# A retention layer feeding a feed-forward block: the halves of the last output slice loaded one place later, their casts moved behind two turned chunks, and products moved ahead of transposes

## The chip, the cores and the metric

The kernel runs on one core of one Trainium2 chip. The metric is device time in microseconds. Before the change the median of three runs is 191.54 us (191.42, 191.54 and 193.94 us). One further execution was profiled: it took 192.3 us, of which 190.5 us lie between its first and its last instruction (the span). All rows of a trace count from the start of that span.

## The reference

The first half is a recurrent attention over 768 steps, for 4 batches of 8 heads of width 64; the second is a feed-forward block over the 3072 resulting tokens.

```
state = gamma * state + outer(k[t], v[t])      # per batch and head, gamma = 1 - 2**(-5-h)
y[t]  = q[t] @ state / sqrt(64)
h     = y_tokens @ w_in                        # 3072 x 512 by 512 x 2048
g     = h * tanh(softplus(h))
out   = g @ w_out                              # 2048 x 512, float32 out
```

## The kernel before

The recurrence is done in chunks of 128 steps, numbered 0 to 23 over the four batches. For a chunk the kernel needs its q and k turned so that the head dimension lies on partitions ("qkt"), a product of both ("at", the scores), a mask ("am"), a product with v ("y"), and the state: an outer product of k and v ("u") added to the state of the chunk before ("suc") and decayed ("stc"). Chunks are gathered to blocks: the first block has four, and ten more have two each. For each block the feed-forward's two products follow, and in all blocks after the first both of them use a scheme of seven products instead of eight on quarter matrices, for which sums of operands are formed on VectorE ("xsum", "gsum", "wsum", "tmat").

The program is written in an order by hand: each engine executes its instructions in the order of the calls, and waits on semaphores where an operand or a buffer isn't ready. The place of the change is the end of the first block, the function `first_g2` (lines 1185 to 1307), which computes the first block's second product and, between its pieces, prepares chunks 4 to 7. `CPB` is 4, so `CPB` and `CPB + 1` are chunks 4 and 5, the two of the next block. What the names there mean:

- `mm(...)` in `first_g2` is four matmuls of 128 by 128 by 256 (line 1210). `pe[p]`, `px[p]`, `pz[p]`, `pb[p]` are accumulators in PSUM for the two token pairs p = 0 and 1; `sm(p, i)` are sums of activations, `t(i)` sums of weights, `a(p, i, s)` activations, `b(s, j)` output weights.
- `turn(g, True)` (line 449) transposes q and then k of chunk g by TensorE, four transposes each (lines 453 and 455), into a PSUM tile of the pool "at", and copies the tile out on ScalarE (line 458).
- `outer_fifth(CPB)` (line 599) is eight small matmuls for chunk 4's outer product (line 604) and an addition on VectorE (line 608); `decay_of_fifth` (line 610) is four small activations on ScalarE (line 614).
- `cast_wout(3, ...)` (line 209) casts a half of the last slice of output weights on ScalarE (line 214). The slice's halves are loaded by `load_last_wout` (line 194, 512 KB each) in `load_more`; the other loads there are q and v of chunks 5 to 7 (line 157, 256 KB each). All are issued by SyncE on one queue.
- k of a chunk is loaded by GpSimd's queue with a cast on the way (`bring_k`, lines 415 and 418); GpSimd also scales q (line 406) and v (line 423).
- `some_late(n)` takes the next n of a list of sums of output weights on VectorE (lines 722 to 725).
- `scores`, `mask` and `y_two` (lines 469, 565, 640 and 622) finish chunks 4 and 5; `end` (line 1275) multiplies with the last slice of output weights.

The PSUM pool "at" has two buffers, used in turn: both turned chunks, the outer product of chunk 4, the scores of 4 and of 5, y, each takes the next one, and waits until its last reader is done.

Of the kernel before, what the change touches and what calls it, by code (L numbers as in the profile page):

```python
# [16 lines left out]
def kernel(  # L17
# [176 lines left out]
    def load_last_wout(half):  # L194
        f = slice(half * (FPS // 2), (half + 1) * (FPS // 2))
        nc.sync.dma_start(
            wtmps["out", NSL - 1][:, f], wout_ap[:, NFB - FPS + f.start:NFB - FPS + f.stop])
# [11 lines left out]
    def cast_wout(s, f, on_act=False):  # L209
        if s not in wouts:  # L210
            wouts[s] = cpool.tile([P, FPS, d_model], FP16, name=f"wout{s}")
        dst, src = wouts[s][:, f], wtmps["out", s][:, f]
        if on_act:
            nc.scalar.copy(dst, src)
        else:
            nc.vector.tensor_copy(dst, src)
# [204 lines left out]
    def cast_v(g):  # L421
        if g < NCK:
            nc.gpsimd.tensor_tensor(  # L423
                room16(g)[2], loaded[g][2], vs.unsqueeze(2).broadcast_to((P, H, D)), op=ALU.mult)
# [24 lines left out]
    def turn(g, on_act=False):  # L449
        q16, k16 = cast[g][:2]  # L450
        t_ps = atps.tile([P, H, C], FP16, name="t_ps", tag="at")
        for i in range(HP):
            nc.tensor.transpose(t_ps[:, i], q16[:, 2 * i:2 * i + 2], ident)
        for i in range(HP):
            nc.tensor.transpose(t_ps[:, HP + i], k16[:, 2 * i:2 * i + 2], ident)
        qkt = qktp.tile([P, H, C], FP16, name="qkt", bufs=4)
        if on_act:
            nc.scalar.copy(qkt, t_ps)
        else:
            nc.vector.tensor_copy(qkt, t_ps)  # L460
        qkts[g] = (qkt[:, :HP], qkt[:, HP:])

    def scores(g):
        at = ats[g] = atps.tile([P, 2, HP, C], FP32, name="at", tag="at")
        qt, kt = qkts[g]
        for i in range(HP):
            for hh in range(2):
                o = 64 * hh
                nc.tensor.matmul(  # L469
                    at[:, hh, i], kt[o:o + 64, i], qt[o:o + 64, i],  # L470
                    start=True, stop=True)
# [127 lines left out]
    def outer_fifth(g):  # L599
        _, k16, v16, _ = cast[g]  # L600
        u_ps = u_tile()[:, 0, :, :D]
        for i in range(HP):
            for x in range(2):
                nc.tensor.matmul(
                    u_ps[64 * x:64 * x + 64, i], k16[:, 2 * i + x], v16[:, 2 * i + x],
                    start=i == 0, stop=True, skip_group_check=True)
        sus[g] = stp.tile([P, HP, D], FP32, name="suc", tag="suc")
        nc.vector.tensor_tensor(sus[g], u_ps, stcs[g - 1], op=ALU.add)

    def decay_of_fifth():  # L610
        stcs[CPB] = stp.tile([P, HP, D], FP16, name="stc", tag="stc")
        su = sus.pop(CPB)
        for i in range(HP):
            nc.scalar.activation(stcs[CPB][:, i], su[:, i], AF.Copy, scale=gcf[:, i:i + 1])
# [426 lines left out]
        load_one(CPB + 1, 0, nc.sync)  # L1041

    def load_more():
        load_last_wout(0)
        load_one(CPB + 1, 2, nc.sync)
        load_last_wout(1)
        nload[0] += 2
        room(CPB + 2)
        load_one(CPB + 2, 2, nc.sync)
        load_one(CPB + 2, 0, nc.sync)  # L1050
        nload[0] += 1
        load_to(CPB + 4)
# [132 lines left out]
    def first_g2():  # L1185
        hf = d_model // 2
        pairs = range(CPB // 2)
        t1 = [mmps.tile([P, 2, hf], FP32, name="o_ps", tag="mm") for _ in pairs]
        t0 = [mmps.tile([P, 2, hf], FP32, name="o_ps", tag="mm") for _ in pairs]
        osb = [[op.tile([P, 2, hf], FP32, name="osb", tag="osb") for _ in range(2)] for _ in pairs]  # L1190
        m5 = [op.tile([P, hf], FP32, name="snap", tag="snap", bufs=4) for _ in pairs]
        pb, pe = [t[:, 0] for t in t0], [t[:, 1] for t in t0]
        px, pz = [t[:, 0] for t in t1], [t[:, 1] for t in t1]
        sums = gsums[0].rearrange("p s (f a) t -> p s f (a t)", a=2)

        def a(p, i, s):
            return lambda f: gts[0, s * FPS + f][:, (2 * p + i) * P:(2 * p + i + 1) * P]

        def sm(p, i):
            return lambda f: sums[:, i - 1, f, p * P:(p + 1) * P]  # L1200

        def b(s, j):
            return lambda f: wouts[s][:, f, j * hf:(j + 1) * hf]

        def t(i):
            return lambda f: tmats[(i - 1) // 2][:, (i - 1) % 2, f]

        def mm(o_ps, x, w, first=False, last=False):
            for f in range(FPS):
                nc.tensor.matmul(  # L1210
                    o_ps, x(f), w(f), start=first and f == 0, stop=last and f == FPS - 1,
                    skip_group_check=True)

        for p in pairs:
            mm(px[p], a(p, 0, 0), b(0, 0), True)
            nc.scalar.copy(osb[p][0][:, 0], px[p])
        cast_wout(1, slice(3, 4), True)
        room_for_more()
        for p in pairs:
            mm(pe[p], sm(p, 1), t(1), True)  # L1220
            nc.scalar.copy(m5[p], pe[p])
        cast_wout(2, slice(0, 2))
        cast_wout(2, slice(2, 4), True)
        some_late(1)
        gate(tmats[0][:, 1, 0, :1])
        cast_q(CPB)
        cast_q(CPB + 1)
        cast_v(CPB)
        some_late(1)
        g_sum(4)  # L1230
        some_late(1)
        for p in pairs:
            mm(pz[p], a(p, 1, 1), b(1, 1))
        for p in pairs:
            mm(pb[p], a(p, 0, 1), b(1, 0))
        for p in pairs:
            mm(pb[p], a(p, 0, 2), b(2, 0))
        for p in pairs:
            mm(pe[p], a(p, 0, 1), b(1, 1))
        for p in pairs:  # L1240
            mm(px[p], sm(p, 2), t(2))
            nc.scalar.copy(osb[p][0][:, 1], px[p])
        turn(CPB, True)
        for p in pairs:
            mm(px[p], sm(p, 3), t(3))
            nc.vector.tensor_tensor(osb[p][1][:, 1], px[p], m5[p], op=ALU.add)
        bring_k(CPB + 2)
        cast_v(CPB + 1)
        cast_wout(3, slice(0, 2), True)
        for p in pairs:  # L1250
            mm(pe[p], sm(p, 4), b(2, 1))
            if p == 0:
                turn(CPB + 1, True)
        outer_fifth(CPB)
        some_late(1)
        decay_of_fifth()
        cast_wout(3, slice(2, 4), True)
        for p in pairs:
            mm(px[p], a(p, 1, 1), b(1, 0))
        scores(CPB)  # L1260
        scores(CPB + 1)
        mask(CPB)
        mask(CPB + 1)
        some_late(2)
        for p in pairs:
            mm(px[p], a(p, 1, 2), t(4))
        cast_v(CPB + 2)
        bring_k(CPB + 3)
        cast_q(CPB + 2)
        turn_by_dma(CPB + 2)  # L1270
        load_early_v(CPB + 4)

        def end(p, i, half):
            for f in range(2 * half, 2 * half + 2):
                nc.tensor.matmul(  # L1275
                    (t0, t1)[i][p], a(p, i, 3)(f), wouts[3][:, f], start=False,
                    stop=f == FPS - 1, skip_group_check=True)

        def ended(p, i):
            if i == 0:  # L1280
                nc.vector.tensor_tensor(osb[p][0], t0[p], osb[p][0], op=ALU.add)
            else:
                works = [
                    lambda: nc.vector.tensor_tensor(
                        osb[p][1][:, 1], pz[p], osb[p][1][:, 1], op=ALU.add),
                    lambda: nc.scalar.copy(osb[p][1][:, 0], px[p])]
                for work in works:
                    work()
            row0 = (2 * p + i) * P
            stores.append((1, out[row0:row0 + P], osb[p][i].rearrange("p j c -> p (j c)")))  # L1290

        ends = [(p, i) for p in pairs for i in range(2)]
        for p, i in ends:
            end(p, i, 0)
        for p, i in ends:
            if (p, i) == (0, 1):
                y_two(1)
            end(p, i, 1)
            if (p, i) == (0, 1):
                midway_of_seventh(CPB + 2)  # L1300
            if p == 0:
                ended(p, i)
            if (p, i) == ends[0]:
                some_late(1)
        x_sums(FIRST, lambda: state_sum(CPB + 2))
        last_ended.extend(ends[2:])
        last_ended.append(ended)
# [111 lines left out]
```

## Time and profile before

| what | value |
|---|---|
| median of three runs | 191.54 us |
| profiled execution, its whole time | 192.3 us |
| its span, first to last instruction | 190.5 us |
| TensorE busy (PE) | 183.4 us, 96% of the span |
| VectorE busy (DVE) | 156.2 us, 82% |
| ScalarE busy (ACT) | 127.2 us, 67% |
| GpSimd busy (POOL) | 95.6 us, 50% |
| DMA moved | 36.17 MB, mean 190 GB/s |

A row of the timeline gives the start in us, the time from the first start to the last end of a run of equal instructions, the engine, the line, the operation, what it writes and reads, shapes, their count, and in brackets how long the engine stood idle before it and on what. Since matmuls are pipelined, eight in a row whose row says 1.04 us hold up the next one by less than that; the chain of waits, whose pieces don't overlap, gives the time that each adds. SPq rows are SyncE's issues of transfers, and their times are those of the issue, not of the transfer.

### The profile page before, as it was taken

To read this page: it belongs to the slowest core of one execution; us is meant where nothing else is said; L and a number is where in the kernel's file an instruction comes from. 1 tells how busy PE (TensorE), PEld (TensorE's weight loads), DVE (VectorE), ACT (ScalarE), POOL (GpSimd) and SP (SyncE) were. 2 spreads that over 40 slices of the span, in tenths; PEclk is the share of its full clock that TensorE was granted. 3 is DMA by queue.
4 is the path that set the end of the run, shared out by engine and by line. 5 is a ranking of instruction groups with operands and counts; after the bars stand their busy time and mean duration, and the time that the engine had idled before them with its cause. 6 is when DMAs were issued, how large, how long until landed. Compare 5 with 4: busy or idle time off the path is not lost.

```text
span 190.5 us, 7724 instructions
## 1 busy us (share of the span) xinstructions
PE 183.4 (96%) x3283; PEld 156.1 (82%) x3283; DVE 156.2 (82%) x329; ACT 127.2 (67%) x249; POOL 95.6 (50%) x135
## 2 busy tenths in 40 slices
PE   7889999989999999999999999999999999999992
PEld 3457546865988998998988988988988988989981
DVE  3996899859899699797897897797897897796672
ACT  3462599482894793794794883883883974975960
POOL 6570107696586947933943944925925923000000
PEclk9999999999999999999999999999999999999999
DMA  5999999998899999999998996993996993300203
GB/s 168 351 370 405 406 405 272 250 251 124 118 203 242 146 265 220 202 238 234 173 188 142 148 186 196 189 253 65 184 173 121 145 163 59 114 0 6 111 0 110
DMA packets 95521, 36.17 MB, mean 190 GB/s; under 512 B 82560, under 2 KB 88960, under 8 KB 95488
## 3 DMA queue, kind: packets, MB, share of 16 engines
q1 hardware_dynamic: 74112, 32.78, 73.1%
q0 software_dynamic: 21088, 2.62, 21.8%
q8 instruction: 25, 0.41, 0.9%
q10 hardware_dynamic: 288, 0.30, 0.4%
q14 instruction: 8, 0.07, 0.1%
HBM read 27.30 MB, written 6.29 MB: 176 GB/s over the span
## 4 chain that ended last, share of the span: by engine, by line
PE 77%; DMA 14%; SPq 5%; DVE 1%; POOL 1%; issue 1%
PE h_ps L820 34%; PE o_ps L956 32%; DMA qk<-in_k_dram 5%; DMA wi<-in_moe_w_in_dram 5%; DMA wt<-in_moe_w_out_dram 5%; SPq L270 3%; PE o_ps L1275 2%; PE y_ps L532 2%; PE at L497 2%; PE u_ps L483 2%; PE y_ps L543 2%; PE o_ps L1210 1%; SPq L184 1%; DVE osb L977 1%; POOL qk L415 1%
## 5 line engine op out<-in xcount | busy, mean ns | idle before, releaser
L840 DVE TENSOR_TENSOR hsum<-h_ps,hsnap 128x512 f32<-128x512 f32 x60 | 38.5, 685 | 9.8 <-ACT hsnap L830 6.9
L830 ACT COPY hsnap<-h_ps 128x512 f32<-128x512 f32 x60 | 32.2, 591 | 9.8 <-PE h_ps L820 9.7
L820 PEld LDWEIGHTS <-wsum 128*128 128x128 f16 x640 | 36.3, 98 | 0.3 <-issue 0.2
L835 ACT ACTIVATE g<-hsum 128x512 f16<-128x512 f32 x60 | 34.6, 644 | 0.8 <-DVE hsum L840 0.4
L956 PEld LDWEIGHTS <-gsum 128*128 128x128 f16 x320 | 30.5, 98 | 3.7
L820 PE MATMUL h_ps<-xsum,wsum 128*128 128x128 f16 x480 | 30.3, 219 | 0.0
L956 PE MATMUL o_ps<-tmat,gsum 128*128 128x256 f16 x240 | 29.5, 273 | 0.0
L820 PEld LDWEIGHTS <-win 128*128 128x128 f16 x480 | 28.2, 98 | 0.9
L418 POOL DMA_DIRECT2D qk<-in_k_dram x36 | 27.6, 775 | 0.0
L956 PEld LDWEIGHTS <-g 128*128 128x128 f16 x248 | 22.7, 98 | 2.6
L406 POOL TENSOR_TENSOR qk<-qf,qvs 128x512 f16<-128x512 f32 x20 | 22.2, 1112 | 0.0
L423 POOL TENSOR_TENSOR v<-vf,qvs 128x512 f16<-128x512 f32 x20 | 20.7, 1054 | 0.5 <-PE at L469 0.5
L956 PE MATMUL o_ps<-wout,g 128*128 128x256 f16 (+1 forms) x168 | 20.8, 267 | 0.0
L820 PE MATMUL h_ps<-xt,win 128*128 128x128 f16 x320 | 19.6, 219 | 0.0
L550 ACT COPY hsum<-y_ps 128x512 f32<-128x512 f32 x9 | 5.3, 587 | 18.4 <-PE y_ps L543 18.4
L977 DVE TENSOR_TENSOR osb<-o_ps,snap 128x256 f32<-128x256 f32 (+1 forms) x32 | 13.0, 413 | 5.0 <-PE o_ps L956 2.6
L597 POOL TENSOR_TENSOR stc<-suc,gcv 128x256 f16<-128x256 f32 x15 | 9.9, 660 | 13.6 <-DVE suc L592 13.6
L427 POOL COPY gate<-gsum 128x1 f16<-128x1 f16 x10 | 1.9, 187 | 26.8 <-DVE gsum L927 26.1
L965 ACT COPY snap<-o_ps 128x256 f32<-128x256 f32 x31 | 11.4, 372 | 5.5 <-PE o_ps L956 5.3
L820 PE MATMUL h_ps<-xsum,win 128*128 128x128 f16 x160 | 12.3, 220 | 0.0
L820 PE MATMUL h_ps<-xt,wsum 128*128 128x128 f16 x160 | 12.2, 219 | 0.0
L835 ACT ACTIVATE g<-h_ps 128x512 f16<-128x512 f32 x20 | 12.0, 599 | 0.0
(144 smaller groups left out, 311.0 us busy)
## 6 DMA issues: line engine op xcount, KB each, us to landing
vf<-in_v_dram SPq DMA_DIRECT2D x24, 256.0 KB, 5.7
out_dram<-osb SPq DMA_DIRECT2D x22, 256.0 KB, 2.8
qf<-in_q_dram SPq DMA_DIRECT2D x20, 256.0 KB, 5.1
wi<-in_moe_w_in_dram SPq DMA_DIRECT2D x3, 1024.0 KB, 10.6
wt<-in_moe_w_out_dram SPq DMA_DIRECT2D x3, 1024.0 KB, 9.6
qk<-in_k_dram POOLq DMA_DIRECT2D x36, 64.0 KB, 4.5
qfirst<-in_q_dram SPq DMA_DIRECT2D x2, 512.0 KB, 4.3
kf<-in_k_dram SPq DMA_DIRECT2D x4, 256.0 KB, 4.9
```

Of the source, the lines that this page charges most:

```text
L270: nc.sync.dma_start(t, dict(k=k, v=v)[nm][0, half * HP:(half + 1) * HP, s * R * P:(s + 1) * R * P].rearrange("h (p r) d -> p h r d", r=R))
L406: nc.gpsimd.tensor_tensor(by_head(g, room16(g)[0]), by_head(0, loaded[g][0]), f.broadcast_to((P, 2, HP, D)), op=ALU.mult)
L418: nc.gpsimd.dma_start(room16(g)[1][:, x::2], src[:, HP * x:HP * x + HP])
L423: nc.gpsimd.tensor_tensor(room16(g)[2], loaded[g][2], vs.unsqueeze(2).broadcast_to((P, H, D)), op=ALU.mult)
L597: by.tensor_tensor(stcs[g], sus.pop(g), decay, op=ALU.mult)
L820: nc.tensor.matmul(h_ps[g][:, f], w(g, f, d), x(d), start=first and f == 0 and d == 0, stop=d == n - 1, skip_group_check=True)
L830: nc.scalar.copy(x, h_ps)
L835: nc.scalar.activation(gt[:, fb:fb + FPS, j * P:(j + 1) * P], h, AF.Mish, scale=inv_boost3)
L840: nc.vector.tensor_tensor(h, h_ps, x, op=ALU.add)
L956: nc.tensor.matmul(t, x(f), w(f)[:, c], start=first and f == 0, stop=f == n - 1, skip_group_check=True)
L965: nc.scalar.copy(x[:, c], t)
L977: nc.vector.tensor_tensor(dst[:, c], t, plus[:, c], op=ALU.add)
```

## The change

Four things are moved, and nothing is added or taken away.

1. In `load_more`, v of chunk 5 is issued ahead of the two halves of the last output slice, which now stand next to each other; before, it stood between them.
2. The product of `sm(p, 4)` and `b(2, 1)` for pair 0 moves from behind both products of `sm(p, 3)` to ahead of the transposes of chunk 4; for pair 1 it moves from behind chunk 5's transposes to ahead of them.
3. Both casts of the last output slice on ScalarE come after the copy of turned chunk 5, and the second one now ahead of chunk 4's decay instead of behind it.
4. The outer product of chunk 4 moves from behind chunk 5's transposes to between the two products of `a(p, 1, 1)` and `b(1, 0)`; the sum of output weights taken by `some_late(1)` moves ahead of it on VectorE.

```
     def load_more():
-        load_last_wout(0)
         load_one(CPB + 1, 2, nc.sync)
-        load_last_wout(1)
+        for half in range(2):
+            load_last_wout(half)
         nload[0] += 2
...
             nc.scalar.copy(osb[p][0][:, 1], px[p])
+        mm(pe[0], sm(0, 4), b(2, 1))
         turn(CPB, True)
         for p in pairs:
             mm(px[p], sm(p, 3), t(3))
             nc.vector.tensor_tensor(osb[p][1][:, 1], px[p], m5[p], op=ALU.add)
         bring_k(CPB + 2)
         cast_v(CPB + 1)
+        mm(pe[1], sm(1, 4), b(2, 1))
+        turn(CPB + 1, True)
         cast_wout(3, slice(0, 2), True)
-        for p in pairs:
-            mm(pe[p], sm(p, 4), b(2, 1))
-            if p == 0:
-                turn(CPB + 1, True)
-        outer_fifth(CPB)
         some_late(1)
-        decay_of_fifth()
-        cast_wout(3, slice(2, 4), True)
         for p in pairs:
             mm(px[p], a(p, 1, 1), b(1, 0))
+            if p == 0:
+                outer_fifth(CPB)
+        cast_wout(3, slice(2, 4), True)
+        decay_of_fifth()
         scores(CPB)
```

On TensorE, behind chunk 5's transposes, the difference between the two programs reads as follows (a minus is before, a plus is now; L455 are the transposes of k of chunk 5, L604 the outer product of chunk 4, `gsum` the sums of activations, `g` the activations; a product is four such pairs of rows, of which one is shown).

```order
 L455 LDWEIGHTS qk_608
 L455 MATMUL t_ps<-ident,qk_608 128x128
-L1210 LDWEIGHTS gsum
-L1210 MATMUL o_ps<-wout_702,gsum 128x256
...
+L1210 LDWEIGHTS g
+L1210 MATMUL o_ps<-wout_637,g 128x256
...
 L604 LDWEIGHTS qk_605
 L604 MATMUL u_ps<-v_606,qk_605 64x64
```

The product of pair 1 that stood here is ahead of chunk 5's transposes now, and a product with `wout_637` that stood behind the outer product stands in its place.

On ScalarE, from the copies of the first block's output (L1242) to the decay of chunk 4 (L614); `qkt<-t_ps` are the copies of turned chunks 4 and 5, `wout_781` and `wout_800` both name the last output slice, in the one program and in the other:

```order
 L1242 COPY osb<-o_ps 128x256 x2
-L458 COPY qkt<-t_ps 128x1024
-L214 CAST wout_781<-wt 128x1024
-L458 COPY qkt<-t_ps 128x1024
+L458 COPY qkt<-t_ps 128x1024 x2
+L214 CAST wout_800<-wt 128x1024 x2
 L614 ACTIVATE stc<-suc,gcf 128x64 x4
```

The first cast moved from between the two copies to behind them, and the second one, which followed the decay, to ahead of it.

On SyncE, the loads at the end of the first block (L196 the halves of the output slice, the first `vf` below is v of chunk 5, the second one v of chunk 6):

```order
 L157 DMA qf<-in_q_dram 128x8x64
-L196 DMA wt<-in_moe_w_out_dram 128x2x512
 L157 DMA vf<-in_v_dram 128x8x64
-L196 DMA wt<-in_moe_w_out_dram 128x2x512
+L196 DMA wt<-in_moe_w_out_dram 128x2x512 x2
 L157 DMA vf<-in_v_dram 128x8x64
```

The first half went one place back, past v of chunk 5; from v of chunk 6 on the queue is as it was.

## The prediction

> **What bounds the kernel now.** I read the page's busy times and chain first, then the chain of waits in order of time, then each engine's timeline around the change. From the page:
>
> ```profile
> span 190.5 us, 7724 instructions
> PE 183.4 (96%) x3283; PEld 156.1 (82%) x3283; DVE 156.2 (82%) x329; ACT 127.2 (67%) x249; POOL 95.6 (50%) x135
> PE 77%; DMA 14%; SPq 5%; DVE 1%; POOL 1%; issue 1%
> ```
>
> TensorE is busy for 96% of the span, so a change of order can win only from the 7 us that it idles in all. The chain that ended last shows where the idling near the change is; its columns are start, time added, and what.
>
> ```profile
> 30.79 8.83 DMA qk<-in_k_dram
> 39.62 0.05 issue
> 39.66 0.40 PE t_ps L455 x4
> 40.06 0.44 PE o_ps L1210 x4
> 40.50 0.24 PE u_ps L604 x8
> 40.74 0.98 PE o_ps L1210 x8
> 41.72 0.55 PE at L469 x16
> ...
> 43.25 2.16 PE o_ps L1275 x10
> ...
> 45.98 0.45 PE y_ps L622 x12
> ...
> 55.02 0.25 PE u_ps L483 x16
> 55.27 0.42 PE at L497 x32
> ...
> 69.22 0.25 PE u_ps L483 x16
> 69.47 0.26 PE at L497 x32
> ```
>
> The last transfer on which TensorE waits is k of chunk 5: issued by GpSimd at 30.79, landed at 39.62. From there to the end the chain is TensorE's own work, almost without a break, so that what is won or lost at 39.66 moves all that follows. One small break I read from two pairs of rows: an outer product and scores took 0.25 + 0.42 = 0.67 us at 55.02 and 0.25 + 0.26 = 0.51 at 69.22. The 0.16 us between them need a cause, and these rows have one:
>
> ```profile
> 50.91 1.25 SPq L431 DMA_TRANSPOSE qkt<-qk x1
> DMA to landing us min/median/max: 4.4/4.4/4.4
> ```
>
> The first is from SyncE's timeline, the second from the view of the tile for that one transfer: chunk 7's turned q and k land at 50.91 + 4.4 = 55.3, in the middle of those scores. I take the 0.16 us as a wait on it.
>
> TensorE's timeline at the change, where the row's last bracket is the idle time before it:
>
> ```profile
> 38.18 0.60 PE L1210 MATMUL o_ps<-wout,gsum 128*128 128x256 f16 x4
> 38.62 0.39 PE L453 MATMUL t_ps<-ident,qk 128*128 128x128 f16 x4
> 39.66 0.40 PE L455 MATMUL t_ps<-ident,qk 128*128 128x128 f16 x4 [0.66 <-DMA qk<-in_k_dram]
> ```
>
> Before the transfer lands TensorE has done all that the order allows and stands still for 0.66 us. That is the most that the products can fill.
>
> **The products and the transposes.** Nothing is removed: there are as many instructions on every engine. Ahead of k of chunk 5 TensorE now has one product of four matmuls more (pair 1 of `sm(p, 4)`), and behind it one less. The other, pair 0, only changes places with chunk 4's transposes and the products of `sm(p, 3)`, all of which come ahead of the wait in both orders. The chain prices a product at 0.44 us (its row at 40.06). TensorE reached the wait at 39.66 - 0.66 = 39.00; now it reaches it at 39.44. If k still lands at 39.62, transposes still start at 39.66, and 0.44 us of work has gone from behind them: **-0.44 us**. What would be late next are the scores. They need ScalarE's copy of turned chunk 5, and their PSUM buffer is that turned chunk's. ScalarE's timeline:
>
> ```profile
> 37.51 1.01 ACT L458 COPY qkt<-t_ps 128x1024 f16<-128x1024 f16 x1 [0.32 <-PE t_ps L455]
> 38.42 1.05 ACT L214 CAST wout<-wt 128x1024 f16<-128x1024 f32 x1
> 40.10 1.01 ACT L458 COPY qkt<-t_ps 128x1024 f16<-128x1024 f16 x1 [0.63 <-PE t_ps L455]
> 41.24 1.07 ACT L614 ACTIVATE stc<-suc,gcf 128x64 f16<-128x64 f32 x4
> 42.22 1.03 ACT L214 CAST wout<-wt 128x1024 f16<-128x1024 f32 x1
> ```
>
> The copy ends at 41.11. Scores started at 41.72 and would start at 41.28, 0.17 us after it: the cover is thin, and holds. The copy of chunk 4 starts up to 0.44 us later than 37.51, since pair 0's product went ahead of its transposes; it ends by 38.96, while the outer product, which writes into its buffer, starts at 40.50 as before (a product of `a(p, 1, 1)` stands ahead of it in place of one of `sm(p, 4)`). So its addition on VectorE and what follows from it keep their time.
>
> **The casts.** ScalarE's order is now copy, cast, cast, decay from 41.11: by the rows' 1.05, 1.03 and 1.07 us the first half is cast at 42.2, the second at 43.2, the decay done at 44.3. The first half is wanted by the end products at 43.25 - 0.44 = 42.81 (0.6 us of cover), the second by the last two of the ten matmuls, eight of them in, 8/10 of 2.16 us later at 44.5 (1.3 us), the decayed state by the second part of y at 45.98 - 0.44 = 45.5 (1.2 us). Cost **0**, and if the first cover went, each further 0.1 us would cost 0.1. The halves' transfers must be there by 41.1 and 42.2.
>
> ```profile
> 31.40 0.85 SPq L196 DMA_DIRECT2D wt<-in_moe_w_out_dram x1
> 32.81 1.41 SPq L196 DMA_DIRECT2D wt<-in_moe_w_out_dram x1
> DMA to landing us min/median/max: 6.0/7.3/8.6
> ```
>
> From SyncE's timeline and the view of the tile for those two: they landed at 31.40 + 6.0 = 37.4 and 32.81 + 8.6 = 41.4. The bytes ahead of the second half's end are the same in both orders, so I keep 41.4 for it; the first must come no later. v of chunk 5 comes earlier, which nothing waits for.
>
> **VectorE and GpSimd.** These rows of the two timelines carry the effect on the sums that the next block waits for:
>
> ```profile
> 40.78 0.42 DVE L608 TENSOR_TENSOR suc<-u_ps,stc 128x256 f32<-128x256 f32 x1 [1.98 <-PE u_ps L604]
> 41.13 1.27 DVE L722 TENSOR_TENSOR tmat<-wout 128x1024 f16<-128x1024 f16 x1
> 42.32 2.34 DVE L565 TENSOR_TENSOR am<-at,tri 128x1024 f16<-128x1024 f32 x2
> 45.18 1.52 DVE L724 TENSOR_TENSOR tmat<-wout,wout 128x1024 f16<-128x1024 f16 x1
> 49.28 0.29 DVE L786 TENSOR_TENSOR xsum<-xt,xsum 128x256 f16<-128x256 f16 x1
> ```
>
> ```profile
> 38.21 1.04 POOL L423 TENSOR_TENSOR v<-vf,qvs 128x512 f16<-128x512 f32 x1
> 40.77 1.06 POOL L423 TENSOR_TENSOR v<-vf,qvs 128x512 f16<-128x512 f32 x1
> ```
>
> VectorE stood idle for 1.98 us ahead of 40.78 and had no pause of note from there to the last of the xsum at 49.57. The weight sum of line 722 moves into that idle stretch, so the masks begin when scores are there, about 41.28 + half of 0.55 = 41.6 instead of 42.32. The masks, the rest of VectorE's row and the xsum can come up to 0.7 us earlier; they are bound below by y, which TensorE gives 0.44 us earlier. The gate behind the xsum, chunk 7's scaled q and its transposing transfer move with them, by 0.44 to 0.7, and TensorE reaches its scores 0.44 earlier: between 0 and the 0.16 us of that break goes too. Line 722 beside GpSimd's scaling of v took 1.27 us; now it meets the one at 38.21 instead of the one at 40.77, and would delay it, or be delayed, by at most about a microsecond, up to 40.3, where the outer product wants v at 40.50. Cost 0. The page "SBUF — State Buffer" of the Trainium skill, section "Who interferes with whom", says that a VectorE instruction with two SBUF inputs fully blocks against a GpSimd one that reads SBUF, whichever came second. The 1.27 us agree with that; by it the sum of line 722 would end near 39.9, and nothing in my sum is changed.
>
> **The loads.** What none of these rows shows is when k of chunk 5 lands once v of chunk 5 is issued ahead of the half. Both share the DMA engines with it. The nearest rows are the two k transfers themselves (view of the tile, these two issues), and the packets that all queues moved from 31.5 to 33.5 and from 35 to 37:
>
> ```profile
> DMA to landing us min/median/max: 4.4/6.6/8.8
> DMA packets 1919, 0.36 MB, mean 178 GB/s; under 512 B 1919, under 2 KB 1919, under 8 KB 1919
> DMA packets 1295, 0.40 MB, mean 201 GB/s; under 512 B 1196, under 2 KB 1196, under 8 KB 1295
> ```
>
> k of chunk 4, issued just ahead of k of chunk 5, took 4.4 us with only small packets beside it; k of chunk 5 took 8.8 us, part of them beside the half's 2 KB packets. Bounds: were it to go like its forerunner, it would land at 30.79 + 4.4 = 35.2, and TensorE would never wait: it would take the transposes at 39.44 at once, a gain of 0.66. Were it to be served only behind both halves, it would land at 41.4: 41.4 - 39.62 = 1.78 later, less the 0.44: a loss of 1.34. I take the time as before, 39.62, since the bytes moved up to then are the same and its last packets came while those transfers were ending.
>
> **The sum.** -0.44 for the product, -0.16 for the break at 55.3, 0 for the rest: -0.60 us. The profiled execution of 192.3 would become 191.7, with a span of 189.9; off the median of 191.54 the same gives **190.9 us**.
>
> **Rivals.**
>
> *k lands earlier.* If small packets beside it are what let k of chunk 4 through in 4.4 us, then v of chunk 5, whose packets are small, in the half's place lets k of chunk 5 land before 39.4. Then the whole 0.66 goes, with the 0.16: 191.54 - 0.82 = 190.7. For it speaks the pair 4.4 and 8.8; against it that k of chunk 5 was issued behind k of chunk 4 on the same queue, and may have had to wait for that alone. The page "DMA: Bandwidth & Descriptors" of the Trainium skill, section "Queues, rings and completion order", has a DMA engine take turns between its queues by whole packets of several descriptors, so that a turn of large descriptors keeps the other queue out longer. The rows agree as far as they go; by that rule this rival would come true.
>
> *k lands later (slower).* The mechanism is the same queue: v of chunk 5 is many small packets (64 float32 each, by its shape, so 1024 of them against a half's 256 rows of 512), issued at 31.4 ahead of k's bulk. If k's last share on some DMA engine is served behind v and a half, it lands past 39.62 + 0.44 = 40.06, and from that point on each us is a us lost, since all of TensorE's work stands behind those transposes; scores wait with it. At 41.4 it gives 191.54 + 1.34 = 192.9. For it speaks that k's last packets came only when the transfers now reordered were ending; against it that the half, now behind v, was itself the larger thing in the way.
>
> *The gain is taken back.* The chain from xsum to chunk 7's transposing transfer doesn't come earlier, because a later VectorE row or the transfer's own 4.4 us (beside k and q loads) holds it. Then TensorE waits at the scores at 55.3 until then, and all but 0.1 of the gain is gone: 191.4. Against it stand the 0.7 us that VectorE has in hand.
>
> *The change doesn't do what it says.* The rows of each engine stand moved as written, so that only their waits could hide it, for 191.5.
>
> **Chances.** Forecast, around 190.9: 0.42. k earlier, around 190.7: 0.25. The gain taken back, or not there, 191.2 to 191.6: 0.15. k later, 191.6 to 192.9: 0.18. The upper end of the range goes into the last case by about half and so leaves a tenth out there: 192.0. The lower is the full gain, 190.7, less 0.3 for the spread that the two nearest runs and the rounding of rows leave: 190.4. No case comes to 2%, 3.8 us, which is about what a measurement of this kernel can tell from no change: TensorE's idling here is too small, and the worst transfer too near. Faster by over 2%: 0.01; within: 0.97; slower: 0.02.
>
> **What the profile would show.** The idle bracket ahead of k's transposes at 39.66 shrinks from 0.66 to about 0.2 (forecast), vanishes (k earlier), or grows (k later); the chain's transfer ends at 39.6, at under 39.4, or past 40. Scores start near 41.3 with ScalarE's copy ended just before. The masks start near 41.6 and the weight sum of line 722 stands ahead of 40.78. No wait on a cast ahead of line 1275. The scores at 55 take 0.26 and not 0.42, some 0.6 us earlier. The prediction is wrong if k's landing moves by more than half a microsecond, or if a half of the output slice lands past 41.6 and line 1275 begins to wait.

## The result, and the profile after

The changed kernel takes 190.96 us (median of 22 runs, 190.74 to 192.25) against 191.59 us for the kernel before in the same comparison (22 runs, 191.00 to 193.94). The ratio is 0.9971, with a 95% interval of 0.9957 to 0.9984: 0.3% faster, inside what the prediction called no change at 2%, but clear of zero. The forecast was 190.9 us in a range of 190.4 to 192.0. A ratio compares the runs of both kernels that were taken together, without those more than 1.5% above the fastest of their kernel, so it need not equal the quotient of two medians. The two profiled executions lie further apart than the medians, 192.3 and 190.88 us, and the experiments say why.

The page of the kernel after, its first lines and the shares of the chain that ended last:

```profile
span 189.0 us, 7724 instructions
PE 182.5 (97%) x3283; PEld 155.8 (82%) x3283; DVE 155.6 (82%) x329; ACT 126.8 (67%) x249; POOL 95.3 (50%) x135
PE 91%; DVE 3%; DMA 2%; POOL 1%; issue 1%; ACT 0%; SPq 0%; DVEq 0%; POOLq 0%
```

The chain is now TensorE's own for 91% of the span, where it was for 77%: no transfer ends a wait near the change any more. The chain of waits of the kernel after at the same place:

```profile
37.28 0.22 PE t_ps L453 x4
37.50 0.22 PE t_ps L455 x4
37.73 1.31 PE o_ps L1210 x12
39.03 0.22 PE t_ps L453 x4
39.26 0.22 PE t_ps L455 x4
39.48 0.44 PE o_ps L1210 x4
39.92 0.24 PE u_ps L604 x8
40.16 0.54 PE o_ps L1210 x4
40.70 0.55 PE at L469 x16
...
47.05 5.83 PE h_ps L820 x104
52.88 0.87 PE o_ps L956 x8
53.76 0.25 PE u_ps L483 x16
54.01 0.26 PE at L497 x31
```

Chunk 5's k is transposed at 39.26, straight behind its q, and takes 0.22 us there instead of the 0.40 of before: the row of before came straight behind a stop of TensorE, and four transposes that follow a stop took 0.18 us more. Scores start at 40.70 instead of 41.72. At 54.01 the scores of the next block take 0.26 instead of 0.42, so the small break on chunk 7's transposing transfer has gone too.

The transfer of chunk 5's k, by the view of the tile for that one issue, which stands at 30.80:

```profile
DMA to landing us min/median/max: 6.5/6.5/6.5
```

It took 6.5 us, where it took 8.8 before, and landed at 37.3, almost two microseconds before TensorE came for it. So the rival "k lands earlier" is what this execution shows, and not the forecast's 39.62.

ScalarE, VectorE and GpSimd, from their timelines of the kernel after:

```profile
39.52 1.01 ACT L458 COPY qkt<-t_ps 128x1024 f16<-128x1024 f16 x1 [0.74 <-PE t_ps L455]
40.43 2.00 ACT L214 CAST wout<-wt 128x1024 f16<-128x1024 f32 x2
42.32 1.06 ACT L614 ACTIVATE stc<-suc,gcf 128x64 f16<-128x64 f32 x4
```

```profile
38.98 0.87 DVE L722 TENSOR_TENSOR tmat<-wout 128x1024 f16<-128x1024 f16 x1
41.08 2.36 DVE L565 TENSOR_TENSOR am<-at,tri 128x1024 f16<-128x1024 f32 x2 [0.45 <-PE at L469]
43.35 0.68 DVE L723 TENSOR_TENSOR tmat<-wout,tmat 128x1024 f16<-128x1024 f16 x1
43.95 0.68 DVE L724 TENSOR_TENSOR tmat<-wout,wout 128x1024 f16<-128x1024 f16 x1
47.70 0.28 DVE L786 TENSOR_TENSOR xsum<-xt,xsum 128x256 f16<-128x256 f16 x1
```

```profile
44.36 1.17 POOL L406 TENSOR_TENSOR qk<-qf,qvs 128x512 f16<-128x512 f32 x1
```

The casts and the decay run behind the copy without holding anything: nothing ahead of line 1275 waits. The last xsum starts at 47.70 instead of 49.28, 1.58 us earlier, more than TensorE's own 1.02. The rest comes from the masks, which start 1.24 us earlier, and from line 724: 0.68 us instead of 1.52. It started at 43.95, ahead of GpSimd's scaling of chunk 6's q at 44.36; before, it started at 45.18.

### The profile page after: what moved, and what is told of

Same layout as the page of the kernel before. It is cut to its first block, busy times and chain, and to the rows that moved or that the text cites. A ratio compares the mean times of both kernels' runs of the same rounds, so it can differ in the third digit from the quotient of the medians.

```text
span 189.0 us, 7724 instructions
## 1 busy us (share of the span) xinstructions
PE 182.5 (97%) x3283; PEld 155.8 (82%) x3283; DVE 155.6 (82%) x329; ACT 126.8 (67%) x249; POOL 95.3 (50%) x135
## 4 chain that ended last, share of the span: by engine, by line
PE 91%; DVE 3%; DMA 2%; POOL 1%; issue 1%; ACT 0%; SPq 0%; DVEq 0%; POOLq 0%
PE h_ps L820 34%; PE o_ps L956 32%; PE h_ps L687 6%; PE o_ps L1210 5%; DMA qfirst<-in_q_dram 2%; PE h_ps L1057 2%; PE o_ps L1275 2%; PE y_ps L532 2%; PE u_ps L483 2%; PE at L497 2%; DVE am L321 2%; PE y_ps L543 2%; POOL qfirst L249 1%; DVE osb L977 1%; PE at L314 0%
```

## The experiments

Two theories at the start. A: the order of the loads decides when k of chunk 5 lands, and that is most of the gain. B: the product that fills the wait is the gain, and the landing in one profile is an accident. Each chip's runs are compared with runs of the kernel before on that chip, whose median there was 192.2 us.

**The loads alone** (kernel before, with the new `load_more`):

```
-        load_last_wout(0)
         load_one(CPB + 1, 2, nc.sync)
-        load_last_wout(1)
+        for half in range(2):
+            load_last_wout(half)
```

> Only the loads are reordered (v of chunk 5 ahead of both halves of the output slice); products, casts and outer product stand as before. Theory A (the loads decide when k of chunk 5 lands, and that is most of the gain): k lands between 37 and 38.5 instead of 39.62, TensorE has no idle bracket ahead of k's transposes, chunk 5's scores start about 1.0 us earlier than before (41.7 to 40.7), and the time is that of the change, 190.9 to 191.1 (ratio to before 0.996 to 0.998). Theory B (the product that fills the wait is the gain, and the landing in one profile is an accident): k lands at 39.6 or anywhere from 37 to 40, the time stays within 0.1% of before.

Median 191.34 us, ratio 0.9988 (0.9958 to 1.0017). The trace fits A: k landed at 36.99, with no idle bracket. Its chain of waits shows what is left:

```profile
36.84 0.05 issue
36.89 0.40 PE t_ps L453 x4
...
39.04 0.23 PE t_ps L455 x4
...
40.92 0.55 PE at L469 x16
```

Scores start at 40.92 and not at the 40.70 of the whole change. The difference is at chunk 4's transposes, which here come straight behind the products with `sm(p, 2)`, find GpSimd's q not yet scaled, and start after a stop (0.40 instead of 0.22). The time does not bear theory A out: the ratio is above the 0.996 to 0.998 that was expected, and its interval reaches from a gain like the whole change's to none.

**The order alone** (kernel after, with the old `load_more`):

```
-        load_one(CPB + 1, 2, nc.sync)
-        for half in range(2):
-            load_last_wout(half)
+        load_last_wout(0)
+        load_one(CPB + 1, 2, nc.sync)
+        load_last_wout(1)
```

> Only the order of products, casts and outer product is changed; the loads stand as before. Theory A: k of chunk 5 lands near 39.6 as before, the idle bracket ahead of its transposes is about 0.2 instead of 0.66, and the time lies between the two, 0.2 to 0.45 us under before (ratio 0.9977 to 0.999). Theory B: the whole gain of the change, 0.55 to 0.65 us (ratio 0.9965 to 0.9975).

Median 191.94 us, ratio 1.0013 (0.9992 to 1.0035), which neither theory had. k landed at 38.97, as A has it for the old loads, but the k transposes of this order start at 39.15, so there was no wait at all; scores started at 40.76, as early as in the whole change. The time went later in that execution. Its chain has this:

```profile
66.53 6.99 DMA qk<-in_k_dram
73.52 0.04 issue
```

Another transfer of k, for a later chunk, was late at 73.5. Three of the profiles below have such a late wait too, on a chunk's transposing transfer, as here in the loads alone taken a second time:

```profile
75.79 7.11 DMA qkt<-qk
```

It landed at 82.9; in the change's third profile one landed at 83.5, and in that of pair 0 alone at 85.2. So they come with either order of the loads and of the products. From the second block's first product (line 956) to the end, these four executions took 136.8 to 138.3 us, and the others 136.2 to 136.5 (both halves first, which has a wait of its own, aside). The difference, 0.2 to 2.1 us, can cover what the change does at 39.

**The kernel before, profiled once more** (no edit):

> The kernel before, unchanged, profiled once more. If the landing of k of chunk 5 is set by the order of the loads, it lands at 39.62 within 0.3 us again and the idle bracket is 0.5 to 0.9 us. If it differs from one execution to the next (which the spread of before's times, 191.0 to 192.6, would fit), it lands elsewhere by over 0.5 us, and the span follows it us for us.

It took 191.74 us; k landed at 38.90 instead of 39.62, and TensorE did not wait for it. So with the old loads the landing does differ by executions, and falls on either side of the moment when TensorE comes for it. The span of 190.0 us is only 0.5 below the first one's, though the stall, which the table below prices at 0.84 us, was gone. Where the rest went shows in VectorE's and GpSimd's timelines of this run:

```profile
43.67 1.23 DVE L723 TENSOR_TENSOR tmat<-wout,tmat 128x1024 f16<-128x1024 f16 x1
44.83 1.52 DVE L724 TENSOR_TENSOR tmat<-wout,wout 128x1024 f16<-128x1024 f16 x1
```

```profile
44.69 1.11 POOL L406 TENSOR_TENSOR qk<-qf,qvs 128x512 f16<-128x512 f32 x1
```

GpSimd's scaling began at 44.69, line 724 at 44.83, and the latter took 1.52 us. This is a second race, for who starts first, and it became the question of the later runs.

**Both halves ahead of v of chunk 5** (kernel before, otherwise unchanged):

```
-        load_last_wout(0)
+        for half in range(2):
+            load_last_wout(half)
         load_one(CPB + 1, 2, nc.sync)
-        load_last_wout(1)
```

> The kernel before with v of chunk 5 issued behind both halves of the output slice instead of between them. Theory A in the form that the halves' 2 KB packets keep k out: both halves now stand beside k, so it lands later than 39.62, 40 to 41, and the time is 0.4 to 1.2 us above before (192.0 to 192.8). If only what is issued first counts (the first half is first in both), k lands at 39.62 within 0.4 and the time is before's within 0.2%.

Median 193.26 us, ratio 1.0074 (1.0038 to 1.0109). TensorE's timeline:

```profile
38.72 0.39 PE L453 MATMUL t_ps<-ident,qk 128*128 128x128 f16 x4
41.92 0.40 PE L455 MATMUL t_ps<-ident,qk 128*128 128x128 f16 x4 [2.82 <-DMA qk<-in_k_dram]
```

k landed at 41.88 and TensorE stood for 2.82 us; landing and time were both later than expected. This is the cleanest run of the set: one load moved by one place makes the kernel slower by some 1.4 us (0.0074 of 192.2; by the interval, 0.7 to 2.1). GpSimd waited 1.65 us for v of chunk 5 in this profile as well, but the scores, which don't need v, already start 2.16 us later than in the first profile of before. With the other profiles it settles that the order of these loads moves the landing. It is the direction that the halves' large packets would give; that their size is the reason, and not the amount of work queued ahead, no run separated.

**The change, its two halves, and one part undone, on one chip.** The change again, the loads alone again, the order alone again (edits as above), and the change with the weight sum of line 722 back behind the outer product's addition:

```
-        some_late(1)
         for p in pairs:
             mm(px[p], a(p, 1, 1), b(1, 0))
             if p == 0:
                 outer_fifth(CPB)
+                some_late(1)
```

> The changed kernel once more, beside the two halves of the change on one chip. If the order of the loads sets the landing of k of chunk 5, it lands at 37.3 within 0.5 us again, TensorE shows no idle bracket from 36 to 48 and no piece of the chain between 40 and 58 is another engine's. Ratio to before 0.996 to 0.998, and less spread than before: three quarters of its runs within 0.5 us of the fastest.

> The loads alone, again, on the same chip as the whole change. Theory A: k lands at 37.0 within 0.5 us, TensorE's only break near the change is the small one ahead of chunk 4's transposes (0.05 idle and 0.18 of refilling), so the time is 0.2 us (0.1%) above the whole change and 0.35 to 0.45 under before (ratio 0.9977 to 0.9985). Theory B (the products are the gain): within 0.1% of before.

> The order alone, again, on the same chip. Theory A: k lands between 38.9 and 39.7 as in three profiles with the old order of loads; TensorE is at its transposes at 39.1 to 39.4, so the idle bracket is 0 to 0.4 and the time is 0.2 to 0.5 us under before (ratio 0.9975 to 0.999). If the old order of the loads also leaves later transfers late (the look before had the k transfer landing at 73.5 in the chain), there is no gain: ratio 0.999 to 1.002.

> The changed kernel with one part undone: the sum of output weights of line 722 stands behind the outer product's addition on VectorE again. If VectorE's row up to xsum is the next limit, as the masks that began only behind line 722 before suggest, masks start at 41.3 to 41.9 instead of 41.08, the last xsum ends 0.2 to 0.9 us later than 47.98, and the chain shows VectorE or chunk 7's transposing transfer between 44 and 55, with 0.1 to 0.4 us more time than the change. If there is cover enough, xsum is later by up to 0.4 us and the time is the change's within 0.1 us.

Ratios to before: the change 0.9946 (0.9916 to 0.9976), the loads 0.9991 (0.9959 to 1.0022), the order 0.9969 (0.9941 to 0.9997), the sum late 0.9975 (0.9944 to 1.0007). k landed at 37.16, 36.98, 38.16 and 37.14, so that with either order of the products it came earlier with the new loads. The order alone gave 1.0013 in the first set of runs and 0.9969 in this one, on a chip of the same number, so its share stays uncertain by some tenths of a per cent. The loads alone gave 0.9988 and 0.9991, with 1 inside both intervals, and here their median, 191.96 us, is 0.69 above the change's 191.27. That the loads are most of the gain, as theory A has it, is thus not shown by the times. The whole change is under 1 each time.

Several expectations failed. The order alone was to have k at 38.9 to 39.7 and a ratio of 0.9975 to 0.999; both came out lower, the ratio within its interval of what was expected. The loads alone were to gain 0.15% or more and gained 0.09%, with an interval that holds both. The change again was to show no other engine in the chain and half of its spread; six of twelve runs, not nine, lay within half a microsecond of the fastest, and the chain has VectorE:

```profile
40.79 0.35 PE at L469 x8
41.14 0.02 issue
41.16 0.26 DVE am L565
...
43.52 1.13 DVE tmat L723
44.64 1.45 DVE tmat L724
46.09 0.60 DVE osb L1281
46.69 0.60 DVE tmat L725
47.29 0.34 DVE osb L1284
...
48.08 4.36 PE h_ps L820 x72
```

So the changed kernel too loses the second race in some executions; from line 724 the delay runs over VectorE's additions to the output and ScalarE's copy behind them into TensorE's next products. And with line 722 late, the cover was enough in the profiled execution: the masks started at 41.26, the last xsum at 47.81, and all that follows as in the change. The medians, 191.77 against the change's 191.27, don't settle whether that part of the edit is worth anything, since the two intervals overlap.

**GpSimd's scaling taken out of the way** (the change, with one call moved), **the change a third time beside it, and the product of pair 0 alone** (kernel before, with one call moved):

```
         cast_v(CPB + 2)
+        cast_q(CPB + 2)
         bring_k(CPB + 3)
-        cast_q(CPB + 2)
         turn_by_dma(CPB + 2)
```

```
+        mm(pe[0], sm(0, 4), b(2, 1))
         turn(CPB, True)
...
-        for p in pairs:
-            mm(pe[p], sm(p, 4), b(2, 1))
-            if p == 0:
-                turn(CPB + 1, True)
+        turn(CPB + 1, True)
+        mm(pe[1], sm(1, 4), b(2, 1))
```

> The changed kernel with GpSimd's scaling of chunk 6's q moved ahead of its two issues for k of chunk 7, so that it runs at 42.9 to 43.9 beside the masks (one operand in PSUM) and no longer beside the weight sums of lines 723 and 724 at 43.4 to 45.2. Theory: what makes one of two looks at the changed kernel slower by 0.6 us is that line 724 starts after that scaling and is blocked by it (1.52 instead of 0.68 us). Then 723 and 724 take 0.68 each here, the last xsum ends by 48.0, and the median is 0 to 0.4 us under the changed kernel's on this chip. If line 723 is stretched by the k issues themselves, it or 724 takes over 0.9 us again, and nothing is won.

> The changed kernel a third time, as the measure for the one beside it. k of chunk 5 lands at 37.1 within 0.3 us; TensorE has no break from 36 to 40; line 724 takes 0.68 or about 1.5 us, and in the second case TensorE's first product of the second block (line 956) starts 0.57 us later. Ratio to before 0.994 to 0.998.

> The kernel before with one move alone: the product of pair 0 ahead of chunk 4's transposes. Theory: this product fills the wait for GpSimd's scaled q of chunk 4 (0.05 us idle and 0.18 for refilling the array), so that each execution is 0.24 us shorter, from the start of the products with sm(p, 2) to that of the scores 5.73 instead of 5.97 us where k of chunk 5 is late as in the first profile, or 4.9 instead of 5.14 where it is in time. Fastest run 0.2 to 0.3 us under that of before; the median 0.1 to 0.4 us under. Rival: the product only changes places, 5.14 or more, nothing won.

With q scaled first: median 191.07 us, ratio 0.9949 (0.9921 to 0.9976). The change beside it: 191.34 us, 0.9959 (0.9932 to 0.9985). The intervals overlap almost wholly, so that it beats the change is not shown. In its one profile line 724 took 0.68 us, but line 723 took 1.07. The scaling had not gone out of the way altogether; it had moved to the start of line 723:

```profile
43.38 1.07 DVE L723 TENSOR_TENSOR tmat<-wout,tmat 128x1024 f16<-128x1024 f16 x1
```

```profile
42.85 1.04 POOL L406 TENSOR_TENSOR qk<-qf,qvs 128x512 f16<-128x512 f32 x1
```

The scaling ended at 43.89 and line 723 at 44.45, 0.56 us later, much as line 724 ended 0.55 us behind it in the second profile of before (45.80 and 46.35). So this run does not test what the issues for k alone do to line 723. The third profile of the change lost the race again (1.34 and 1.52 us).

Pair 0 alone: median 191.94 us, ratio 0.9975 (0.9948 to 1.0003), fastest run 190.90 against 191.12. Its profiled execution took 194.12 us, more than its other runs, with the loss at the transfer that landed at 85.2; I read it only up to the scores at 55. k was as late as in the first profile:

```profile
38.42 0.39 PE L453 MATMUL t_ps<-ident,qk 128*128 128x128 f16 x4
39.66 0.40 PE L455 MATMUL t_ps<-ident,qk 128*128 128x128 f16 x4 [0.85 <-DMA qk<-in_k_dram]
```

TensorE came to chunk 5's transposes 0.24 us earlier (2.63 us behind the start of the products with `sm(p, 2)`, before 2.87), the gain that was expected of this product, but stood for 0.85 instead of 0.66: with k late, this part is worth 0.05 us (5.86 to the scores against 5.91), where 5.73 was expected.

**The profiles side by side.** All times in us, from the traces. "To scores" and "to line 956" run from the start of the products with `sm(p, 2)` (35.75 before, 35.80 after) to the start of the scores (line 469) and of the second block's first product (line 956), so that small shifts ahead of the change don't count.

| kernel | loads | k lands | idle for k | to scores | lines 723 / 724 | to line 956 |
|---|---|---|---|---|---|---|
| before | old | 39.62 | 0.66 | 5.91 | 0.68 / 1.52 | 18.24 |
| before again | old | 38.90 | none | 5.07 | 1.23 / 1.52 | 17.74 |
| pair 0 alone | old | 39.62 | 0.85 | 5.86 | 0.67 / 1.52 | 18.22 |
| order alone | old | 38.97 | none | 4.83 | 0.89 / 0.68 | 16.91 |
| order alone again | old | 38.16 | none | 4.83 | 0.98 / 0.68 | 16.92 |
| loads alone | new | 36.99 | none | 5.07 | 0.76 / 0.68 | 17.16 |
| loads alone again | new | 36.98 | none | 5.07 | 0.73 / 0.68 | 17.16 |
| after | new | 37.27 | none | 4.83 | 0.68 / 0.68 | 16.92 |
| after again | new | 37.16 | none | 4.83 | 1.21 / 1.52 | 17.48 |
| after, third | new | 36.91 | none | 4.83 | 1.34 / 1.52 | 17.61 |
| sum of line 722 late | new | 37.14 | none | 4.83 | 0.68 / 0.68 | 16.92 |
| q ahead of k | new | 37.32 | none | 4.83 | 1.07 / 0.68 | 16.91 |
| both halves first | halves first | 41.88 | 2.82 | 8.07 | 1.48 / 0.68 | 20.15 |

Three terms can be read from it, each from a few executions. **The order of the loads**: k lands at 36.9 to 37.3 with the new, at 38.2 to 39.6 with the old, at 41.9 with the halves first. TensorE comes for it at about 39, so with the old loads it is sometimes late (two of five profiles), and then costs 5.91 - 5.07 = 0.84 us. **The product ahead of chunk 4's transposes**: 5.07 - 4.83 = 0.24 us, in every profile where k was in time, whatever the loads. **The second race**: where line 724 takes 1.52, line 956 comes 0.56 to 0.69 us later (17.48 and 17.61 against 16.92; 17.74 against 17.16). It was lost in all three profiles with the old loads and the old order of products (in one of them pair 0's had been moved), and in two of three of the change. With k in time, the outcome goes with line 723: where the race was lost, line 723 had taken 1.21 to 1.34 us and was still running when the scaling began, and where it was won, 0.68 to 0.98 (q ahead of k aside, where the scaling had been moved).

## Why the prediction was right, and where it was not

The time, 190.9 against 190.96, and the direction were right. The sum behind it was not the one that the chip made, and part of the agreement is luck. By the sign that the prediction itself had set, a landing of k that moves by more than half a microsecond, its account was wrong: k came 2.35 us earlier.

- **"I take the time as before, 39.62"** failed. k landed at 37.27, and at 36.9 to 37.3 in every profile with these loads. The bounds given (35.2 and 41.4) held it, and the rival "k lands earlier" described it; the reason that I gave for keeping the time, that the bytes moved up to then are the same, did not count. The order in which the loads beside k were issued did. The Trainium skill's "DMA: Bandwidth & Descriptors", section "Queues, rings and completion order", states that a DMA engine takes a whole packet from one queue before it turns to the next; that a turn of large rows keeps k out longer was my inference from it. The landings agree in direction (36.9 to 37.3 with the small packets first, 41.88 with both halves first), though no run changed the size of a packet alone.
- **"-0.44 for the product"** was a term for a wait that is gone. With k at 37 there is no wait at chunk 5's k for the product of pair 1 to fill. What is gained by k in time is 0.84 us in an execution where it had been late, and nothing in one where it had not. The first profile was of the former kind, and I read it as the rule. Of the 1.42 us between the two profiled executions, 1.32 arise ahead of line 956: 0.84 from the stall, 0.24 from the product ahead of chunk 4's transposes, and 0.24 between the scores and line 956, where line 724 took 1.52 us before and 0.68 after. The medians, over executions of all kinds, differ by 0.63.
- **"the most that the products can fill", 0.66 us**, was too small as a price. The stall costs 0.84: the four transposes behind it take 0.40 us in the chain, and 0.22 where they follow without a stop, so 0.18 come on top of the idle bracket. The prediction quoted the 0.40 and did not ask about it.
- **"The other, pair 0, only changes places"**, costed at nothing, is the part of the change that pays in each profile with k in time: 0.24 us, by filling the wait for GpSimd's scaled q at 36.8 and sparing the slower transposes behind it. The rows that I quoted began behind that place. The fastest runs of kernels with it lie at 190.74 to 190.90 us and of those without at 191.02 to 191.19 (before 191.00 to 191.12); the order alone, first time, with 191.44, is the exception.
- **The break at 55.3, -0.16**, was right in size and in its reason, that chunk 7's transposing transfer would come earlier: it was issued at 49.32 instead of 50.91, and the scores took 0.26 us in place of 0.42. But the break is no fixed term either. In the profile of pair 0 alone k was as late as before and the transfer was issued at 50.94, yet it took 4.0 us instead of 4.4, and the break was gone (both halves first, with the transfer at 57.7, has the break again):

```profile
55.30 0.26 PE at L497 x32
```

- **VectorE, "up to 0.7 us earlier"**, was mis-sized: the last xsum came 1.58 us earlier. Line 724 fell from 1.52 to 0.68 us as it got ahead of GpSimd's scaling. I had quoted the 1.52 and not asked what it was; with k in time losing that race costs 0.56 to 0.69 us, as much as the whole measured gain, and it was lost in two of three profiles of the change.
- **Line 722 and the casts at 0** agree with the profiles: no wait at line 1275, and the sum put back changed nothing that follows in its profile. The first half landed 1.2 us later than before, at 38.55, which the prediction had not allowed for, and still ahead of its cast at 40.43. No run moved the casts or the outer product alone.
- **The slower rival** did not come true. That a load beside k can make it late is real all the same: the same load moved the other way costs some 1.4 us. But it was the halves ahead that did it, and not v of chunk 5, as that rival had it.

How the 0.63 us divide stays open. The parts seen in the profiles are the 0.24 us, the share of executions in which k was late, the share in which line 724 was blocked, and the late waits behind 73 us, which come and go with either kernel. Thirteen profiles, three of them of the change, do not give such shares, and the times of the loads alone and of the order alone don't either.

## What to carry to other kernels

One profile of a kernel shows one throw of its races: when a transfer lands close to the moment at which its user arrives, profile the kernel twice before pricing the wait. Issue a transfer that nothing waits for yet behind the one on which the bounding engine will stand, rather than beside it, and try both orders. Look at the places where that engine starts again, since a stall cost more here than its idle time. An instruction that takes more than twice its usual time beside another engine is a term of its own, to be priced before the edit and not after.

## What the runs showed of the hardware that was not expected

Which of VectorE and GpSimd is held up depended on who started first, even by a tenth of a microsecond. Line 724 (two inputs in SBUF) and GpSimd's scaling of chunk 6's q started at 43.95 and 44.36 after, where line 724 took 0.68 and the scaling 1.17; and at 44.57 and 44.46 in the second profile of the change:

```profile
44.57 1.52 DVE L724 TENSOR_TENSOR tmat<-wout,wout 128x1024 f16<-128x1024 f16 x1
```

```profile
44.46 1.08 POOL L406 TENSOR_TENSOR qk<-qf,qvs 128x512 f16<-128x512 f32 x1
```

In all eleven profiles in which the two meet, line 724 takes 0.68 us where it starts first and 1.52 where it starts second; in the five of the second kind the scaling had begun before line 723 was done. The Trainium skill's "SBUF — State Buffer", section "Who interferes with whom", says that a VectorE instruction with two SBUF inputs contends with a GpSimd one that reads SBUF, that the lock is exclusive, and that the order of issue decides who blocks. The traces agree, down to the 0.11 us by which the scaling came first here.

Line 723 shows the same where it starts behind a scaling (1.07 us with q ahead of k, 1.48 with both halves first). What stretches it in the other profiles (0.67 to 1.34 us), in which GpSimd issues transfers for most of its time, stays unexplained; and since the race behind it goes with its length, so does why the changed kernel loses it in some executions.
